# Attention and mixture of experts on one core: waits of TensorE placed ahead of need, the threshold's scalar loaded by GpSimd, ten warming products

## The chip, the cores and the metric

The program runs on one core of one Trainium2 chip, as one launch. The metric is the device time in microseconds (us). Three runs of the kernel before are given, and one profiled execution. An engine is named as in the profile: PE is TensorE (PEld its weight loads), DVE is VectorE, ACT is ScalarE, POOL is GpSimd, SP is SyncE.

## The reference

Attention over 8 batches of 8 heads, 576 tokens of width 64, where scores more than `tau` below the row's maximum are dropped; then a soft mixture of experts over all 4608 tokens (8 experts, 4 slots each, width 512 to 1024 to 512).

```python
scores = scale * np.matmul(q, k.transpose(0, 1, 3, 2))
thresh = np.max(scores, axis=-1, keepdims=True) - tau
scores = np.where(scores >= thresh, scores, -1000000000.0)
attn = softmax(scores)                       # over the keys
x = np.matmul(attn, v)                       # heads side by side: (4608, 512)
logits = x @ phi                             # (4608, 32)
d = softmax(logits, axis=0)                  # over the tokens
slot_input = d.T @ x
slot_out = relu(slot_input @ w1[e]) @ w2[e]  # for each expert e
out = softmax(logits, axis=1) @ slot_out
```

All data is float32.

## The kernel before

**Stages.** At the start, constants are made: GpSimd makes an identity matrix (`ident`, 128x128), SyncE loads the scalar `tau` to all 128 partitions (line 602), and VectorE makes `flag8` (line 604), `nabs` and `pabs` (lines 619 and 621) from it. TensorE multiplies `ident` by itself `UP` = 13 times (line 630); these warming products have no use but to keep TensorE at work while the first data comes in. Then follows the attention, up to about 475 us, and then the experts (lines 1219 and 1254) and the output (lines 1298 and 1304).

**Attention.** The 64 heads go in 32 pairs, four pairs to a batch. For each pair SyncE loads keys, queries and values; of the first pair the halves come from SyncE and ScalarE in turn (lines 745 and 746). The keys are scaled by `flag8` (line 754: VectorE for the first pair, GpSimd later). A pair has nine score rows. For each: TensorE forms 128x576 scores in a PSUM region (`ps`, line 774; the ninth, with the leftover tokens, line 779), VectorE copies them to `ss` and takes the maximum (line 786), ScalarE takes the exponential (line 796), GpSimd the threshold (line 799), VectorE drops what is below it and sums (line 802). Then TensorE transposes the result `p` in pieces of 64 (line 690, `ptr`), ScalarE copies it out to `pTa`, `pTb`, `pTl` (line 695), TensorE multiplies with the values `vv` (line 892), and a turned-back `x` is scaled by GpSimd (line 911) and transposed once more by TensorE (line 916).

**What sets the order.** `Order.add` records each operation with its engine, a planned duration, its needs and its `mode`, the tiling of TensorE's array. `Order.plan` (line 458) simulates the engines from a table of numbers (`TABLE`) and gives every operation a planned start; it also gives out the PSUM regions (four of them) and the buffers. `Order.run` (line 532) then writes the operations in the order of their planned starts, and the program's framework adds the waits: each instruction can carry one wait on a semaphore, and further ones stand in separate rows ahead of it (EVENT_SEMAPHORE in the trace). Before the change all waits of an operation stand at its first instructions. An engine works through its instructions in order.

**Lines of the steps that follow.** The filling products on `ident` in the first pair (line 682) stand among the first score products. The separate waits belong to lines 690, 774, 892 and 916. The operation of line 892 has ten products of 64 rows (256 or 320 columns), that of line 690 mostly sixteen.

Of the kernel before, what the change touches and what calls it, by code (L numbers as in the profile page):

```python
# [10 lines left out]
F32 = mybir.dt.float32  # L11
# [15 lines left out]

HALVES, COLS, COLS4, QUADS, WHOLE = range(5)
SWITCH = 145
PERIOD = 14142.5  # L30

REGIONS = 4
NPRE = 26
UP = 13
WARM = 13
FILL = 14
NHOST = 20
# [362 lines left out]
class Order:  # L400
# [57 lines left out]
    def plan(self, table):  # L458

        ops = self.ops  # L460
        n = len(ops)
        nom = [base * PERIOD / 9 + table.get((name, k), rel * PERIOD / 9) for name, k, base, rel in self.noms]
        left = [len(o[3]) for o in ops]
# [19 lines left out]
        while any(queue.values()):  # L483
# [33 lines left out]
            if eng == "PE":  # L517
                end += SWITCH * (o[5] != mode) + 50 * (free[eng] < t)
                mode = o[5]
# [12 lines left out]
    def run(self, tc):  # L532
        start, slot = self.plan(TABLE)
        self.start = start
        pool = tc.alloc_tile_pool(name="ps", bufs=1, space=PSUM)
        banks = [pool.tile([128, 2, 512], F32, name=f"ps{i}") for i in range(REGIONS)]
        for i in sorted(range(len(start)), key=lambda i: (start[i], i)):
            for b in self.ops[i][4]:
                if b.t is None:
                    k = slot[b]  # L540
                    if b.kind in "sw":
                        b.t = banks[k[0]] if b.kind == "s" else banks[k[0]][:, 0]
                    else:
                        b.t = self.slots[b.kind][k]
            self.ops[i][2]()
        pool.release()
        return slot


@with_exitstack  # L550
def softmax_attention_soft_moe(
# [17 lines left out]
    nc = tc.nc  # L569
# [13 lines left out]
    cp = ctx.enter_context(tc.tile_pool(name="consts", bufs=1))  # L583
    wp = ctx.enter_context(tc.tile_pool(name="weights", bufs=1))
    att = ExitStack()


    ident = cp.tile([128, 128], F32, name="ident")
    make_identity(nc, ident)
    st1 = cp.tile([128, 32], F32, name="st1")  # L590
    nc.vector.tensor_reduce(
        out=st1, in_=ident.rearrange("p (g s) -> p s g", g=4), axis=AX.X, op=ALU.add
# [5 lines left out]
    nc.vector.memset(ones_left[0:64], 0.0)  # L598
    nc.vector.memset(ones_left[64:128], 1.0)
    phi_sb = cp.tile([128, HP, NS], F32, name="phi_sb")  # L600
    tau_sb = cp.tile([128, 1], F32, name="tau_sb")
    nc.sync.dma_start(tau_sb, tau.to_broadcast([128, 1]))
    flag8 = cp.tile([128, 1], F32, name="flag8")
    nc.vector.tensor_scalar(
        out=flag8, in0=tau_sb, scalar1=0.0, scalar2=0.125, op0=ALU.is_ge, op1=ALU.mult
# [21 lines left out]
    with tc.tile_pool(name="ps_up", bufs=1, space=PSUM) as up:  # L627
        t = up.tile([128, 512], F32, name="up")
        for i in range(UP):
            nc.tensor.transpose(out=t[:, i % 4 * 128:i % 4 * 128 + 128], in_=ident, identity=ident)  # L630
# [7 lines left out]
        d=([128, 2, 4, NS], F32), M=([128, 2], F32), f=([128, 1], F32),  # L638
# [19 lines left out]
    n = NPRE + NHOST  # L658
# [459 lines left out]
    start, first_plan = G.plan(TABLE)  # L1118
    slot = first_plan
    users = {}  # L1120
# [3 lines left out]
    end = lambda c: max(start[k] + G.ops[k][1] for k in users[c])  # L1124
# [8 lines left out]
    for i in range(NHOST):  # L1133
        n = next(n for n in reversed(range(len(cells))) if sum(map(bytes_of, cells[n:])) >= (i + 1) * 4096)
        G.add("SP", 1350, NP * N9 + 9, lambda n=n, i=i: host(n, i),
              after=sorted({users[c][-1] for c in cells[n:] if c in users} | {k for c in cells[n:] for k in users.get(c, ()) if k >= recent[-3]}))
    with tc.manual_schedule():
        slot = G.run(tc)
# [182 lines left out]
    end = [None, None]  # L1321
# [75 lines left out]
```

## Time and profile before

| what | value |
|---|---|
| three runs | 546.73, 546.8, 548.49 us (median 546.8) |
| profiled execution | 546.92 us |
| its span, first to last instruction | 545.1 us |
| mean granted clock of TensorE | 0.992 |
| scores, line 774, on TensorE | 166.7 us, 1024 matmuls of 429 ns |
| values, line 892, pTb / pTa / pTl | 76.0 / 62.3 / 41.9 us |
| transpositions of p, line 690 | 98.0 us, 2304 of 223 ns |
| separate waits on TensorE at lines 774, 690, 892, 916 | 74, 59, 32, 28 |

A busy time is the sum over the instructions of a group, and "idle before" is the time that the engine stood still ahead of them. In the timeline each row has its start, how long it lasts, the engine, the line, the operation, and output and input; in brackets stands the idle time before it and what ended it. "SPq" and "ACTq" are the queues' issues of transfers.

### The profile page before, as it was taken

The numbers are of one execution on the slowest core, as the hardware profiler recorded it, in microseconds if no ns is written. First come the engines' busy times: TensorE is split into PE (matmuls) and PEld (weight loads), VectorE is DVE, ScalarE is ACT, GpSimd is POOL, SyncE is SP. The second block draws the span as 40 slices with busy tenths as digits, with TensorE's granted clock in tenths as the row PEclk, the third lists the DMA queues.
The fourth block names the chain that finished last, engine by engine and source line by source line (L and its number), as shares of the span: only waits on it lengthen the run. The fifth ranks groups of instructions, "written<-read, shape, count | busy, mean of one in ns | idle before, by whom it ended". The sixth has DMA issues, their size and how long they took to land.

```text
span 545.1 us, 18237 instructions
## 1 busy us (share of the span) xinstructions
PE 524.6 (96%) x7016; PEld 339.9 (62%) x7016; DVE 473.8 (87%) x1333; ACT 459.5 (84%) x789; POOL 234.1 (43%) x475
## 2 busy tenths in 40 slices
PE   8999999999999999999999999999999999999990
PEld 6666666666666666666766666666666666644470
DVE  6999999999999999999999999998999999623192
ACT  3999998999899989999999989998999989611181
POOL 2554544554345444553455435554564445021030
PEclk9999999999999999999999999999999999999996
DMA  6433335557472738275424333333334223899598
GB/s 154 92 90 92 96 90 189 162 161 182 118 214 85 215 91 244 60 211 129 130 66 117 90 91 93 91 91 92 83 76 114 52 53 130 334 408 407 207 372 320
DMA packets 31990, 83.03 MB, mean 152 GB/s; under 512 B 4640, under 2 KB 12832, under 8 KB 31904
## 3 DMA queue, kind: packets, MB, share of 16 engines
q1 hardware_dynamic: 31584, 81.43, 49.1%
q8 instruction: 55, 0.90, 0.7%
q10 hardware_dynamic: 320, 0.44, 0.3%
q14 instruction: 31, 0.25, 0.1%
HBM read 72.42 MB, written 9.44 MB: 150 GB/s over the span
## 4 chain that ended last, share of the span: by engine, by line
PE 77%; DVE 7%; ACT 6%; DMA 4%; issue 3%; SPq 0%; DVEq 0%; POOL 0%; POOLq 0%; ACTq 0%
PE ps L892 27%; PE ps L774 22%; PE ps L690 16%; PE ps L779 3%; ACT p L796 2%; PE ps L916 2%; DVE ss L786 2%; DMA host<-in_w 2%; DMA w<-in_w 2%; DVE p L802 2%; PE ps L1022 2%; PE ps L974 2%; PE h L1219 1%; ACT pTa L695 1%; DVE host L1308 1%
## 5 line engine op out<-in xcount | busy, mean ns | idle before, releaser
L786 DVE TENSOR_SCALAR_CACHE_REDUCE ss<-ps 128x576 f32<-128x576 f32 x288 | 208.4, 752 | 12.4 <-issue 3.7
L802 DVE SCALAR_TENSOR_TENSOR p<-ss,thr,p 128x576 f32<-128x576 f32 x256 | 206.4, 836 | 2.3 <-POOL thr L799 1.4
L796 ACT ACTIVATE p<-ss,nmx 128x576 f32<-128x576 f32 x256 | 187.5, 775 | 11.0 <-DVE ss L786 10.0
L799 POOL TENSOR_SCALAR thr<-nmx,pabs 128x1 f32<-128x1 f32 x288 | 121.1, 425 | 158.4 <-DVE ss L786 148.8
L774 PE MATMUL ps<-k,q 64*128 64x288 f32 x1024 | 166.7, 429 | 0.7 <-issue 0.2
L774 PEld LDWEIGHTS ps<-k,q 64*128 64x128 f32 x1024 | 84.5, 189 | 25.9 <-ACT pTb L695 4.8
L690 PEld LDWEIGHTS ps<-ident,p 64*128 64x128 f32 x2304 | 88.9, 138 | 18.1 <-DVE ss L786 2.9
L690 PE MATMUL ps<-ident,p 64*128 64x64 f32 x2304 | 98.0, 223 | 0.4 <-ACT pTl L874 0.2
L695 ACT COPY pTb<-ps 128x1024 f32<-128x1024 f32 (+1 forms) x96 | 83.4, 877 | 2.8 <-PE ps L690 2.1
L892 PE MATMUL ps<-pTb,vv 128*64 128x320 f32 x512 | 76.0, 439 | 0.0
L695 ACT COPY pTa<-ps 128x1024 f32<-128x1024 f32 x64 | 64.9, 1015 | 1.3 <-PE ps L690 1.0
L892 PE MATMUL ps<-pTa,vv 128*64 128x256 f32 x512 | 62.3, 385 | 0.2 <-ACT pTa L695 0.2
L892 PEld LDWEIGHTS ps<-pTb,vv 128*64 128x64 f32 x512 | 33.9, 136 | 32.7 <-issue 3.9
L892 PEld LDWEIGHTS ps<-pTa,vv 128*64 128x64 f32 x512 | 33.9, 136 | 25.2 <-DVE ss L786 6.2
L911 POOL TENSOR_TENSOR x<-x,ri 128x512 f32<-128x512 f32 x31 | 34.8, 1122 | 20.0 <-ACT x L695 19.8
L892 PE MATMUL ps<-pTl,vv 128*64 128x256 f32 (+1 forms) x256 | 41.9, 406 | 0.0
L833 POOL TENSOR_SCALAR pL<-pL,ri 128x576 f32<-128x576 f32 x31 | 24.4, 788 | 27.4 <-DVE ri L829 14.5
L695 ACT COPY xT<-ps 128x256 f32<-128x256 f32 (+1 forms) x62 | 24.7, 401 | 5.3 <-PE ps L892 3.5
L802 DVE SCALAR_TENSOR_TENSOR pL<-ss,thr,pL 128x576 f32<-128x576 f32 x32 | 26.1, 816 | 1.5 <-ACT pL L796 1.4
L892 PEld LDWEIGHTS ps<-pTl,vv 128*64 128x64 f32 x256 | 18.4, 137 | 12.7
L695 ACT COPY pTl<-ps 128x256 f32<-128x256 f32 x64 | 23.9, 374 | 2.5 <-PE ps L690 1.8
L754 POOL TENSOR_SCALAR k<-k,flag 128x576 f32<-128x576 f32 x31 | 24.7, 797 | 2.9 <-DMA k<-in_kT 1.7
(166 smaller groups left out, 532.3 us busy)
## 6 DMA issues: line engine op xcount, KB each, us to landing
w<-in_w SPq DMA_DIRECT2D x44, 512.0 KB, 8.4
q<-in_qT SPq DMA_DIRECT2D x62, 288.0 KB, 4.5
vv<-in_vt SPq DMA_DIRECT2D x32, 320.0 KB, 4.2
host<-in_w SPq DMA_DIRECT2D x20, 512.0 KB, 8.5
k<-in_kT SPq DMA_DIRECT2D x62, 144.0 KB, 3.4
out<-w SPq DMA_DIRECT2D x8, 512.0 KB, 3.4
out<-host SPq DMA_DIRECT2D x8, 512.0 KB, 5.1
out<-host SPq DMA_DIRECT2D x4, 256.0 KB, 4.5
```

The source lines that it names most:

```text
L690: nc.tensor.transpose(out=s[:, g, c:c + 64], in_=ins[g], identity=ident[rows[g], rows[g]], tile_position=(64 * g, 0))
L695: G.add("ACT", 51 + 0.833 * n, nom, lambda: nc.scalar.copy(*io()), r, w)
L754: sc = lambda e, kc=kc: lambda: e.tensor_scalar(out=kt.t[:, kc], in0=kt.t[:, kc], scalar1=flag8, **one)
L774: nc.tensor.matmul(s.t[:, g, 0:HS], qt.t[rows[g], h, c * 128:(c + 1) * 128], kt.t[rows[g], h * HS:(h + 1) * HS], start=True, stop=True, ti ...
L779: nc.tensor.matmul(s.t[rows[a], g, 0:HS], qt.t[rows[g], a, SM:S], kt.t[rows[g], a * HS:(a + 1) * HS], start=True, stop=True, tile_position ...
L786: dve(674, t + OFF['mx'], [s], [ss, nmx], lambda s=s, ss=ss, nmx=nmx: nc.vector.tensor_scalar(out=ss.t.rearrange("p (a k) -> p a k", a=2), ...
L796: G.add("ACT", 668, t + OFF['ex'], lambda sv=sv, nmx=nmx, view=view: nc.scalar.activation(view().rearrange("p (a k) -> p a k", a=2), sv(), ...
L799: pool(250, t + OFF['th'], lambda nmx=nmx, thr=thr: nc.gpsimd.tensor_scalar(out=thr.t, in0=nmx.t, scalar1=1.0, scalar2=pabs, op0=ALU.mult, ...
L802: fn=lambda sv=sv, thr=thr, view=view, i=i: nc.vector.scalar_tensor_tensor(out=view().rearrange("p (a k) -> p a k", a=2), in0=sv(), scalar ...
L833: pool(725, t + OFF['sc'], lambda k=k, view=view_: nc.gpsimd.tensor_scalar(out=view(), in0=view(), scalar1=ri.t[:, k:k + 1], **one), [ri[c ...
L892: nc.tensor.matmul(lone(w)[h * 64:(h + 1) * 64, 0:n], vv.t[:, v0:v0 + 64], p0, start=(kb == 0), stop=(kb == 4), tile_position=(0, h * 64), ...
L911: G.add("POOL", 1040, u + 6.8, own=f"new{j}" + group(b), r=[ri[0]], w=[x[j]], fn=lambda: nc.gpsimd.tensor_tensor(out=wide(), in0=wide(), i ...
```

## The change

Three parts. First, `run` now asks a new function, `early`, for waits that are to be taken ahead. For each operation of TensorE it collects the latest need on each other engine and each load, together with the users of the PSUM region or buffer that it takes over. Of these all but the last by plan (all, if a load is among them) may move to one of the eight operations of TensorE before it, the nearest that qualifies: one of at least 400 ns in the plan, with tiling HALVES or COLS, not a score operation, whose middle lies at least 400 ns (3500 for a load) after the planned end of the producer. In that host the wait is put on the third instruction or the next free ones, up to four. Second, the scalar `tau` is loaded by GpSimd as its first work, ahead of `ident`; SyncE's load of it is gone. Third, `UP` is 10.

```diff
+REACH = 8
-UP = 13
+UP = 10
...
     def run(self, tc):
...
-        for i in sorted(range(len(start)), key=lambda i: (start[i], i)):
+        order = sorted(range(len(start)), key=lambda i: (start[i], i))
+        early = self.early(start, slot, order)
+        made, made_of = [], {}
+        nc = tc.nc
+        nc.push_inst_callback(made.append)
+        for i in order:
...
+            del made[:]
             self.ops[i][2]()
+            made_of[i] = [x.name for x in made]
+            at = [x for x in made][2:]
+            for d in early.get(i, ()):
+                names = made_of[d] if self.ops[d][0] == "SP" else made_of[d][-1:]
+                for name in names:
+                    if at:
+                        tc.add_manual_dep(
+                            at.pop(0), name,
+                            mybir.DependencyInfo(mybir.DependencyClass.Sync, mybir.DependencyReason.DATA),
+                            reason="waited for ahead of the operation that needs it")
+        nc.pop_inst_callback()
...
+    def early(self, start, slot, order):
+
+        ops = self.ops
+        pos = {i: n for n, i in enumerate(order)}
+        end = [start[i] + ops[i][1] for i in range(len(ops))]
+        users = {}
+        for i in order:
+            for b in ops[i][4]:
+                users.setdefault(b, []).append(i)
+        behind, there = {}, {}
+        for i in order:
+            for b in ops[i][4]:
+                if b.kind is not None and users[b][0] == i:
+                    unit = ("ps", slot[b][0]) if b.kind in "sw" else (b.kind, slot[b])
+                    if unit in there:
+                        behind.setdefault(i, []).extend(users[there[unit]])
+                    there[unit] = b
+        seen = {}
+        pe = [i for i in order if ops[i][0] == "PE"]
+        out = {}
+        for n, i in enumerate(pe):
+            need = {}
+            for d in [*ops[i][3], *behind.get(i, ())]:
+                e = ops[d][0]
+                if e == "PE":
+                    continue
+                if e == "SP":
+                    if d not in seen:
+                        need["SP", d] = d
+                elif pos[d] > seen.get(e, -1) and pos[d] > pos.get(need.get(e), -1):
+                    need[e] = d
+            late = sorted(need.values(), key=lambda d: end[d])
+            for d in late if any(ops[d][0] == "SP" for d in late) else late[:-1]:
+                margin = 3500 if ops[d][0] == "SP" else 400
+                for h in reversed(pe[max(0, n - REACH):n]):
+                    if ops[h][1] < 400 or ops[h][5] not in (HALVES, COLS) or ops[h][1] in (488, 494):
+                        continue
+                    if pos[d] < pos[h] and end[d] + margin < start[h] + ops[h][1] / 2 and len(out.get(h, ())) < 4:
+                        out.setdefault(h, []).append(d)
+                        break
...
+    tau_sb = cp.tile([128, 1], F32, name="tau_sb")
+    nc.gpsimd.dma_start(tau_sb, tau.to_broadcast([128, 1]))
     ident = cp.tile([128, 128], F32, name="ident")
     make_identity(nc, ident)
...
-    tau_sb = cp.tile([128, 1], F32, name="tau_sb")
-    nc.sync.dma_start(tau_sb, tau.to_broadcast([128, 1]))
```

The order of the products, copies and loads stays what it was on every engine, but for the scalar's load, the three products, and `pabs`, which now stands behind the scaling of the first keys. Three places show what moved. The first is GpSimd's first work, before:

```order
L1383 MEMSET const-uint8-127 128x1
masks.py:197 MEMSET ident 128x128
masks.py:199 ISA
masks.py:199 AFFINE_SELECT ident<-ident 128x128 [waits Pool_49]
L799 TENSOR_SCALAR thr_230<-nmx_290,pabs 128x1 [waits DVE_49]
```

and now (the line numbers are those of the changed file):

```order
L1448 MEMSET const-uint8-127 128x1
L654 DMA tau_sb<-in_tau 128x1
masks.py:197 MEMSET ident 128x128
masks.py:199 ISA
masks.py:199 AFFINE_SELECT ident<-ident 128x128 [waits Pool_49]
L864 TENSOR_SCALAR thr_227<-nmx_287,pabs 128x1 [waits DVE_49]
```

The scalar's load stands ahead of the identity, whose last step releases the warming products. The second place is TensorE around 99.4 us of the profile, in the second batch: the values' product, the transposition of `x` behind it, and the next ones. Before:

```order
L892 MATMUL ps_328<-pTb_194,vv_190 64x320 [waits Activation_49]
L892 MATMUL ps_328<-pTb_194,vv_190 64x320 x7
L892 MATMUL ps_328<-pTl_198,vv_190 64x320 x2
L916 MATMUL ps_326<-ident,x_142 128x64 [waits DVE_49,Pool_49]
L916 MATMUL ps_326<-ident,x_142 128x64 x7
```

and now, the same work (line 957 is what line 892 was, and 981 is 916):

```order
L957 MATMUL ps_325<-pTb_191,vv_187 64x320 [waits Activation_49]
L957 MATMUL ps_325<-pTb_191,vv_187 64x320
L957 MATMUL ps_325<-pTb_191,vv_187 64x320 [waits DVE_49]
L957 MATMUL ps_325<-pTb_191,vv_187 64x320 x5
L957 MATMUL ps_325<-pTl_195,vv_187 64x320 x2
L981 MATMUL ps_323<-ident,x_139 128x64 [waits Pool_49]
L981 MATMUL ps_323<-ident,x_139 128x64 x7
```

The wait for VectorE, which reads the PSUM region that the transposition takes over, has moved from the transposition to the third of the ten products before it. The third place follows a microsecond later: the first score product with a new pair's keys and queries. Before:

```order
L690 MATMUL ps_325<-ident,p_266 128x64 [waits Activation_49]
L690 MATMUL ps_325<-ident,p_266 128x64 x15
L774 MATMUL ps_328<-k_254,q_258 128x288 [waits DMAHW1_49,DMAHW0_49,Activation_49]
L774 MATMUL ps_328<-k_254,q_258 128x288 [waits DMAHW2_49]
L774 MATMUL ps_326<-k_254,q_258 128x288 [waits Activation_49]
```

and now (line 755 is what line 690 was, and 839 is 774):

```order
L755 MATMUL ps_322<-ident,p_263 128x64 [waits Activation_49]
L755 MATMUL ps_322<-ident,p_263 128x64
L755 MATMUL ps_322<-ident,p_263 128x64 [waits DMAHW7_49]
L755 MATMUL ps_322<-ident,p_263 128x64 [waits DMAHW0_49]
L755 MATMUL ps_322<-ident,p_263 128x64 [waits DMAHW1_49]
L755 MATMUL ps_322<-ident,p_263 128x64 [waits DMAHW7_49]
L755 MATMUL ps_322<-ident,p_263 128x64 x10
L839 MATMUL ps_325<-k_251,q_255 128x288 [waits Activation_49]
L839 MATMUL ps_325<-k_251,q_255 128x288
L839 MATMUL ps_323<-k_251,q_255 128x288 [waits Activation_49]
```

The waits for loads (DMAHW) have moved into the transposition ahead of the scores, one to a product. In the whole listing TensorE has 785 products that wait before and 961 now, and of these 204 carried more than one wait before and 83 now.

More of the change, by code (lines that the diff above doesn't have):

```diff
@@ L546, in run @@
+        nc.pop_inst_callback()
         pool.release()
         return slot
+    def early(self, start, slot, order):
[37 more added lines that the diff above has]
+                        break
+            for d in need.values():
+                if ops[d][0] == "SP":
+                    seen[d] = True
+                else:
+                    seen[ops[d][0]] = max(seen.get(ops[d][0], -1), pos[d])
+        return out
```

## The prediction

> **What bounds the kernel now.** I read the page first, then the chain of work that ended last, then who waited for whom.
>
> ```profile
> span 545.1 us, 18237 instructions
> ...
> PE 524.6 (96%) x7016; PEld 339.9 (62%) x7016; DVE 473.8 (87%) x1333; ACT 459.5 (84%) x789; POOL 234.1 (43%) x475
> ...
> PE 77%; DVE 7%; ACT 6%; DMA 4%; issue 3%; SPq 0%; DVEq 0%; POOL 0%; POOLq 0%; ACTq 0%
> ```
>
> ```profile
> PE ps L779 <- ACT pTl L874: 1.8, 5, 0.4
> ```
>
> TensorE is busy for 96% of the span and carries 77% of the chain, so time that TensorE loses in the attention part is lost to the kernel, and only time that it now loses can be won. The list of waits names little of that: the longest entry for a TensorE product is 1.8 us in five pieces, where the 64x64 products of line 779 wait for a ScalarE copy. That wait comes last where it stands, and the change does not touch its producer.
>
> The first 9 us are another matter, since there nothing else runs yet. The timeline of the start, and the first link of the chain:
>
> ```profile
> 0.73 0.20 POOL masks.py:197 MEMSET ident<- 128x128 f32 x1 [0.29 <-POOLq L1383]
> 0.73 0.40 SPq L602 DMA_DIRECT2D tau_sb<-in_tau  x1
> ...
> 1.01 0.29 POOL masks.py:199 TENSOR_SCALAR_AFFINE_SELECT ident<-ident 128x128 f32<-128x128 f32 x1
> ...
> 1.19 0.58 SPq L745 DMA_DIRECT2D k<-in_kT  x1
> ...
> 1.36 3.04 PE L630 MATMUL up<-ident 128*128 128x128 f32 x13 [1.36 <-POOL ident masks.py:199]
> 1.81 0.59 SPq L746 DMA_DIRECT2D q<-in_qT  x1
> ...
> 2.44 0.60 SPq L745 DMA_DIRECT2D k<-in_kT  x1
> ...
> 3.33 0.15 DVE L604 TENSOR_SCALAR flag<-tau_sb 128x1 f32<-128x1 f32 x1 [1.71 <-DMA tau_sb<-in_tau]
> ...
> 4.11 0.37 DVE L754 TENSOR_SCALAR k<-k,flag 128x288 f32<-128x288 f32 x1 [0.32 <-DMA k<-in_kT]
> ...
> 4.46 0.69 PE L682 MATMUL ps<-ident 128*128 128x128 f32 x2
> ...
> 5.23 2.37 PEld L774 LDWEIGHTS ps<-k,q 64*128 64x128 f32 x12 [0.49 <-issue]
> ...
> 6.31 0.37 DVE L754 TENSOR_SCALAR k<-k,flag 128x288 f32<-128x288 f32 x1 [1.83 <-DMA k<-in_kT]
> ...
> 6.88 0.75 DVE L786 TENSOR_SCALAR_CACHE_REDUCE ss<-ps 128x576 f32<-128x576 f32 x1
> ```
>
> ```profile
> 2.44 3.77 DMA k<-in_kT
> 6.96 1.42 DVE ss L786 x4
> ```
>
> The chain begins with the keys of the second half, issued by SyncE at 2.44 and landed at 2.44 + 3.77 = 6.21. VectorE scales them at 6.31, sums the identity, and starts the first maximum at 6.88. TensorE's first score products start at 5.23, just after the two filling products (4.46 + 0.69 = 5.15). So three paths reach the start together: SyncE's loads, the warming products, and the threshold's scalar (flag at 3.33, scaled keys at 4.11).
>
> **The separate waits.** A product can carry one wait; where it needs more, a row of its own (EVENT_SEMAPHORE) stands ahead of it. By line:
>
> ```profile
> L774 PEldq EVENT_SEMAPHORE  x74: 51/51/1348, 5.2 to 449.8; - x74
> ...
> L892 PEldq EVENT_SEMAPHORE  x32: 51/51/716, 18.6 to 464.9; - x32
> ...
> L916 PEldq EVENT_SEMAPHORE  x28: 51/51/51, 32.2 to 452.6; - x28
> ...
> L690 PEldq EVENT_SEMAPHORE  x59: 51/51/51, 22.1 to 470.8; - x59
> ```
>
> Nearly all take 51 ns. In the program's listing 204 products had several waits, now 83: 121 lose the row ahead of them, and at most 121 x 0.051 = 6.2 us could go with it. Does such a row cost the product behind it anything? The same operation, pTa's product with vv, once followed by a transposition that has one wait (76.21) and once by one that has two (105.80):
>
> ```profile
> 76.21 1.95 PE L892 MATMUL ps<-pTa,vv 128*64 128x256 f32 x16
> ...
> 78.52 0.65 PE L690 MATMUL ps<-ident,p 64*128 64x64 f32 x14
> ```
>
> ```profile
> 105.80 1.95 PE L892 MATMUL ps<-pTa,vv 128*64 128x256 f32 x16
> ...
> 108.11 0.52 PE L690 MATMUL ps<-ident,pL 64*128 64x64 f32 x10
> ```
>
> From start to start it is 78.52 - 76.21 = 2.31 and 108.11 - 105.80 = 2.31 us. The row is worked off while older products still run. So I cost the removed rows at **nothing**; the work that hides them is the long operation in front, and if that cover were gone it would be 51 ns each. Only rows whose own wait comes last cannot be hidden, and the rule keeps most of those: it moves a wait only where the plan has the producer done 0.4 us before the host's middle. The changed listing still has two waits, of ScalarE and GpSimd, on many transpositions of pL.
>
> **What the earlier waits cost.** A wait now stands on the third product of a host operation, and everything behind it on TensorE stands still until it is met. The critical place is the one shown in the listing above, which returns in each batch: L916 needs VectorE's maximum, and that wait moves to the third product of the L892 operation before it.
>
> ```profile
> 99.11 0.75 DVE L786 TENSOR_SCALAR_CACHE_REDUCE ss<-ps 128x576 f32<-128x576 f32 x1
> 99.79 0.08 DVE L786 DVE_READ_ACCUMULATOR ss<-ps 128x1 f32 x1
> ```
>
> ```profile
> 99.70 0.14 PEld L892 LDWEIGHTS ps<-pTb,vv 128*64 128x64 f32 x2
> ```
>
> ```profile
> 99.38 2.37 PE L892 MATMUL ps<-pTb,vv 128*64 128x320 f32 x16
> 101.59 0.71 PE L892 MATMUL ps<-pTl,vv 128*64 128x320 f32 x4
> 102.23 0.46 PE L916 MATMUL ps<-ident,x 64*128 64x64 f32 x8
> ```
>
> VectorE ends at 99.79 + 0.08 = 99.87; the weight load of the third product started at 99.70, so it comes 0.17 us later. The pairs of matmuls stand (101.59 - 99.38) / 8 = 0.28 us apart, so the load runs that far ahead of its matmul and most of the 0.17 is cover. Bounds: 0, and 0.17 with nothing hidden; I take **0.05 us**, near the lower end, because the pitch of this row is the larger number. Eight batches make 0.4 us, bounds 0 and 1.4. A gain below nothing would need the separate rows to cost something, which the 2.31 against 2.31 excludes here. The other moved waits are mostly loads of k and q, whose producers ended long before.
>
> **The start.** Taken from SyncE's queue, the scalar's issue frees 1.19 - 0.73 = 0.46 us: keys and queries that SyncE issues move up by as much, the second half's keys from 2.44 to 1.98, and with them the scaling at 6.31 and the maximum at 6.88. Against that GpSimd now issues a transfer before it makes the identity. No row shows GpSimd issuing one. Bounds: 0, and the whole time from issue to landing of this transfer; the nearest row is SyncE's issue of the same bytes, 0.40 us, and I take that, d = **0.40**.
>
> ```profile
> tau_sb<-in_tau SPq DMA_DIRECT2D x1, 0.5 KB, 2.6
> ```
>
> ```profile
> L630 PE MATMUL up<-ident x13: 421/421/477, 1.4 to 4.0; 128*128 128x128 f32 x13
> ```
>
> The warming products start at 1.36 + d. All 13 take 3.04 us and the last of them 0.42, so they start (3.04 - 0.42) / 12 = 0.22 apart, and three fewer save 0.65. The filling products then end at 5.15 - 0.65 + d, and the first score product can load 0.08 later as before: 4.58 + d = 4.98 instead of 5.23, **-0.25 us**. The scalar would land at 0.73 + d + 2.6 = 3.7; the flag (0.15) and the scaling of the first keys (0.37) behind it end near 4.4, which the warming still hides, the more since the changed program scales the first keys ahead of pabs. At d = 0 the loads decide, -0.46, SyncE's share; at d = 2.6 it is +1.95. The page DMA: Bandwidth & Descriptors of the Trainium skill (section Specifications) gives the path through GpSimd about 1 us to the first byte and that of SyncE about 0.6; with its 1 us as d the first score product would start at 5.58, +0.35. No run here shows it yet.
>
> **Sum.** -0.25 + 0.4 = +0.15 us against the profiled execution's 546.92 (its span is 545.1; the rest lies around it, and the median of the three runs is 546.8): **547.1 us**, no change. Less than 0.3%, 1.64 us, cannot be told from no change.
>
> **The rivals.**
> 1. *The separate rows are in the way after all.* Then up to 6.2 us go: 540.7; a third of it passes the bound. For it speaks that there are so many and that they stand on the busiest engine; against it the two equal 2.31. Chance 0.15.
> 2. *The identity comes late (slower).* Place: GpSimd's first work. Past d = 0.65 every further 0.1 us puts TensorE's first score product 0.1 us later. With the 0.4 of the hosts it passes 1.64 us from d = 0.65 + 1.24 = 1.89; at the upper bound of 2.6 the time is 546.9 + 1.95 + 0.4 = 549.3. For it speaks that nothing else can run on GpSimd meanwhile, against it the 0.40 of the nearest row. Chance 0.07.
> 3. *The change does not take waits off but adds stalls.* The plan's times choose the hosts, not the chip's. With nothing hidden, 8 x 0.17 = 1.4, and the smaller places as much again: 549.3 to 549.7 with all of them, 548.7 with half. Against it: the load's lead. Chance 0.06.
> 4. *TensorE's clock opens later.* The score products of the start need twice the time of the next ones:
>
> ```profile
> 5.20:7.30 2.10, 2.04 (x8) 2.07 (x10) 1.00 0.94 250
> 8.30:9.50 1.20, 1.15 (x8) 0.69 (x8) 1.00 0.94 243
> ```
>
> Eight matmuls in 2.04 us, then eight in 1.15, while both windows show a granted clock of 1.00. A later first product can lengthen the slow stretch, and each us of it loses about half a us. One of the three runs lies 548.49 - 546.73 = 1.76 above the lowest; one such step would give 546.9 + 1.8 = 548.7. Chance 0.05. The page TensorE: Matmul & The Clock Gate of the Trainium skill (Part 1: The HAM clock gate) says that the clock opens at the end of a busy window of about 3.4 us that runs by itself; an estimate by it is 1.7 us for one window more. The halved rate agrees with it; no run here shows the windows.
>
> **How the numbers follow.** Forecast 0.67, rivals 0.15, 0.07, 0.06, 0.05. Faster by over 0.3% is the first rival, 0.15; slower are the other three, 0.18; the same is 0.67. The range begins at 545.0, where part of the first rival still lies, and ends at 548.7, which takes in the clock's step and half of the stalls; the full gain and the late identity are left out.
>
> **What would show it.** The separate rows on lines 774 and 892 gone, and still 2.31 us from L892 to the next operation: the first term is right; a smaller step speaks for the first rival. A gap in the weight loads of the third product near 99.9: the second term, its size against 0.05. The start of the first warming product gives d; the first score product should start near 5.0, the first maximum before 6.88. Wrong would be a first score product after 5.9, or a batch whose length, from one L892 row to the same one of the next batch, has changed by over 0.1 us.

## The result and the profile after

Seven runs of each kernel, medians 553.01 us (548.25 to 555.61) after and 547.07 us (546.56 to 548.87) before: the ratio is 1.0088, with a 95% interval of 1.0062 to 1.0114. The change makes the kernel slower by 5 to 6 us, and 547.1 was forecast with 548.7 as the upper end.

The profiled execution of the changed kernel is the shortest of its seven, 548.25 us. Its page, span, busy times, the chain by engine, and the one new queue:

```profile
span 546.5 us, 18103 instructions
PE 524.5 (96%) x7013; PEld 337.3 (62%) x7013; DVE 473.7 (87%) x1333; ACT 459.3 (84%) x789; POOL 233.3 (43%) x476
PE 74%; DMA 9%; ACT 6%; DVE 4%; issue 3%; POOL 1%; SPq 0%; DVEq 0%; POOLq 0%; ACTq 0%
q0 software_dynamic: 32, 0.00, 0.0%
```

TensorE's busy time has not moved (524.6 before). What has grown is the DMA part of the chain, from 4 to 9%. Most of the rows ahead of the products are gone as meant, 216 before and 86 now: by line, with their counts,

```profile
L839 PEldq EVENT_SEMAPHORE  x6: 51/51/51, 5.9 to 450.0; - x6
L755 PEldq EVENT_SEMAPHORE  x48: 51/51/51, 58.5 to 471.1; - x48
L957 PEldq EVENT_SEMAPHORE  x1: 51/51/51, 465.9 to 465.9; - x1
```

against 74 (now line 839), 59 (755) and 32 (957) before. The timeline of TensorE and of its weight loads at the places that the prediction measured (line 957 is what line 892 was):

```profile
75.69 1.95 PE L957 MATMUL ps<-pTa,vv 128*64 128x256 f32 x16
...
78.00 0.71 PE L755 MATMUL ps<-ident,p 64*128 64x64 f32 x16
```

```profile
105.30 1.95 PE L957 MATMUL ps<-pTa,vv 128*64 128x256 f32 x16
...
107.61 0.53 PE L755 MATMUL ps<-ident,pL 64*128 64x64 f32 x10
```

```profile
98.87 2.38 PE L957 MATMUL ps<-pTb,vv 128*64 128x320 f32 x16
101.08 0.71 PE L957 MATMUL ps<-pTl,vv 128*64 128x320 f32 x4
101.72 0.46 PE L981 MATMUL ps<-ident,x 64*128 64x64 f32 x8
```

```profile
99.42 1.27 PEld L957 LDWEIGHTS ps<-pTb,vv 128*64 128x64 f32 x12 [0.35 <-DVE ss L851]
```

From 75.69 to 78.00 it is still 2.31 us, but this place had one wait before and has one now. The place that had a separate row is the second: before, the row stood at 106.17 and the step was 2.31 us; now the trace has no row there, and from 105.30 to 107.61 it is 2.31 us again. At 99.42 the third product's weight load waits 0.35 us for VectorE's maximum, and yet the operation takes 101.72 - 98.87 = 2.85 us, as before (102.23 - 99.38): the wait is hidden whole.

The start, in the timeline:

```profile
0.74 0.60 SPq L810 DMA_DIRECT2D k<-in_kT  x1
...
1.26 0.74 POOL L654 DMA_DIRECT2D tau_sb<-in_tau  x1 [0.81 <-POOLq L1448]
...
2.00 0.22 POOL masks.py:197 MEMSET ident<- 128x128 f32 x1
...
2.64 2.40 PE L695 MATMUL up<-ident 128*128 128x128 f32 x10 [2.64 <-POOL ident masks.py:199]
...
6.05 1.45 PE L839 MATMUL ps<-k,q 64*128 64x288 f32 x9 [0.26 <-DMA q<-in_qT]
...
7.05 0.74 DVE L851 TENSOR_SCALAR_CACHE_REDUCE ss<-ps 128x576 f32<-128x576 f32 x1
```

GpSimd begins the scalar's load 0.53 us after it could begin the identity before (0.73), and issues it for 0.74: the identity is later by 2.00 - 0.73 = 1.27 us. The first score product starts at 6.05 instead of 5.23, the first maximum at 7.05 instead of 6.88.

TensorE's products come in the same order in both kernels, so I paired them one by one, counted from the end, and took the difference of their starts. In this execution it is -0.6 us at 25 us (the trace's clock record begins, at full speed, at 5.7 us here and at 7.3 before), and it then loses 0.3 at 177.6, 0.3 at 422 and about 0.9 in the experts' part, to 1.4 at the end. That is not the loss of the other six runs. A second profile was needed.

### The profile page after: what moved, and what is told of

It is laid out like the page before. It is cut to its first block, busy times and chain, and to the rows that moved or that the text cites. A ratio compares the mean times of both kernels' runs of the same rounds, so it can differ in the third digit from the quotient of the medians.

```text
span 546.5 us, 18103 instructions
## 1 busy us (share of the span) xinstructions
PE 524.5 (96%) x7013; PEld 337.3 (62%) x7013; DVE 473.7 (87%) x1333; ACT 459.3 (84%) x789; POOL 233.3 (43%) x476
## 4 chain that ended last, share of the span: by engine, by line
PE 74%; DMA 9%; ACT 6%; DVE 4%; issue 3%; POOL 1%; SPq 0%; DVEq 0%; POOLq 0%; ACTq 0%
PE ps L957 26%; PE ps L839 23%; PE ps L755 16%; DMA host<-in_w 4%; DMA w<-in_w 4%; PE ps L844 3%; PE ps L981 2%; ACT p L861 2%; PE ps L1039 1%; PE ps L1087 1%; DVE ss L851 1%; ACT pTa L760 1%; DVE host L1373 1%; DMA vv<-in_vt 1%; DVE cT L1276 1%
## 5 line engine op out<-in xcount | busy, mean ns | idle before, releaser
L864 POOL TENSOR_SCALAR thr<-nmx,pabs 128x1 f32<-128x1 f32 x288 | 119.8, 421 | 159.2 <-DVE ss L851 149.8
L839 PEld LDWEIGHTS ps<-k,q 64*128 64x128 f32 x1024 | 83.4, 188 | 26.3 <-ACT pTb L760 4.9
```

Source lines behind the costliest of these rows:

```text
L839: nc.tensor.matmul(s.t[:, g, 0:HS], qt.t[rows[g], h, c * 128:(c + 1) * 128], kt.t[rows[g], h * HS:(h + 1) * HS], start=True, stop=True, ti ...
L864: pool(250, t + OFF['th'], lambda nmx=nmx, thr=thr: nc.gpsimd.tensor_scalar(out=thr.t, in0=nmx.t, scalar1=1.0, scalar2=pabs, op0=ALU.mult, ...
```

## The experiments

The kernels are taken in three groups of four, each group beside new runs of the kernel before, whose medians are 547.56, 547.47 and 547.96 us. A ratio is that of a kernel to the kernel before of its group, with its 95% interval.

### The changed kernel once more

No edit.

> The changed kernel once more, for a second profile: the one there is (548.25 us) lies 4 to 7 us below the other six runs of the same kernel, so it does not show where most of the loss is. Every theory expects a median near 553. Theory A (the start): GpSimd's first transfer took 1.27 us before the identity in the first profile; in the other runs it takes some 5 us more, so the first score product starts near 11 instead of 6.05 us, and everything behind it is shifted by the same amount. Theory B (the waits): the start is as before, and the loss adds up in the attention part, in steps where a product of a long operation waits. Theory C (the weight stream): start and attention are as before up to 470 us, and the products of the last part wait 5 us longer for their weights.

553.8 us, ratio 1.0113 (1.0088 to 1.0139), and the profiled run is 554.29. The page's span, and from the waits of TensorE the first row; then TensorE's timeline:

```profile
span 552.4 us, 18103 instructions
...
PE ps L755 <- DMA vv<-in_vt: 3.2, 2, 2.5
```

```profile
176.96 0.47 PE L755 MATMUL ps<-ident,pL 64*128 64x64 f32 x10
177.26 0.35 PE L755 MATMUL ps<-ident,p 64*128 64x64 f32 x6
180.09 1.01 PE L755 MATMUL ps<-ident,p 64*128 64x64 f32 x14 [2.48 <-DMA vv<-in_vt]
181.03 1.24 PE L844 MATMUL ps<-k,q 64*64 64x288 f32 x8
```

The same place in the kernel before:

```profile
177.60 0.79 PE L690 MATMUL ps<-ident,p 64*128 64x64 f32 x20
178.32 0.71 PE L779 MATMUL ps<-k,q 64*64 64x288 f32 x8
178.97 1.95 PE L892 MATMUL ps<-pTa,vv 128*64 128x256 f32 x16
```

An operation of twenty transpositions stops after six, for a load of values that no transposition reads. Before, that wait stood at the product with vv, 178.97 - 177.60 = 1.37 us later. The windows around it (engines' busy time, then the granted clock, the DMA share and GB/s):

```profile
170.00:177.50 7.50, 7.50 (x102) 4.95 (x100) 6.98 (x21) 7.36 (x12) 5.04 (x9) 1.00 0.66 203
177.50:180.00 2.50, 0.11 (x4) 0.00 (x0) 2.50 (x9) 2.45 (x6) 1.34 (x4) 0.98 1.06 235
180.00:182.50 2.50, 2.41 (x24) 1.42 (x26) 0.78 (x3) 1.73 (x3) 0.00 (x0) 0.50 0.67 186
182.50:185.00 2.50, 2.50 (x20) 1.32 (x16) 1.34 (x4) 0.00 (x0) 0.69 (x1) 0.84 0.03 13
```

TensorE stands still, and when it goes on the clock is at 0.50: the trace's clock record has one stretch of 3.41 us at half speed here. So the place costs twice. By pairs of products against the profile of before: start -0.45; the stop 2.75; the half clock 1.35; a stop of the same kind at 239 us (vv again, 0.69 in the waits) 0.88; two steps of 0.12; the experts' part 2.2; the rest to the last instruction 0.36. Together 7.3 us, the difference of the spans (552.4 - 545.1). Theory A falls (the start even gained), B and C have a part each.

### One part alone

The waits alone: `UP` and the scalar's load are put back.

```diff
-UP = 10
+UP = 13
...
-    tau_sb = cp.tile([128, 1], F32, name="tau_sb")
-    nc.gpsimd.dma_start(tau_sb, tau.to_broadcast([128, 1]))
...
+    tau_sb = cp.tile([128, 1], F32, name="tau_sb")
+    nc.sync.dma_start(tau_sb, tau.to_broadcast([128, 1]))
```

> The waits taken ahead alone; the scalar stays with SyncE, 13 warming products. Theory A: 546.5 to 547.5, as before. Theory B: 551 to 553. Theory C, if the scalar's queue is the cause: as before. The prediction's own terms for this part: +0.4 (547.3).

549.35 us, 1.0033 (1.0016 to 1.0050): above theory A's range and below theory B's, and 2 us above the prediction's own 547.3. TensorE stands still for vv at 178 here too, 0.9 us.

GpSimd's load alone, in the kernel before:

```diff
+    tau_sb = cp.tile([128, 1], F32, name="tau_sb")
+    nc.gpsimd.dma_start(tau_sb, tau.to_broadcast([128, 1]))
     ident = cp.tile([128, 128], F32, name="ident")
...
-    nc.sync.dma_start(tau_sb, tau.to_broadcast([128, 1]))
```

> The scalar's load by GpSimd alone, 13 warming products, no waits ahead. Theory A: 551 to 554, with the first warming product some 5 us later in those runs. Theory B: d = 1.27 less the 0.46 of SyncE and not the 0.65 of the warming, about 547.5 to 548. Theory C: 551 to 553, and the products of line 1219 or its counterpart wait for weights.

547.36 us, 0.9999 (0.9984 to 1.0015): nothing, though the first warming product comes 1.28 us later (2.64).

Ten warming products alone, in the kernel before:

```diff
-UP = 13
+UP = 10
```

> 10 warming products instead of 13, nothing else. All three theories: 546.5 to 547, since the first score products wait for the queries that land at 5.1. If the clock opens a window later with less warming: 548 to 549.

548.2 us, 1.0017 (1.0006 to 1.0028): the second case of the expectation, a clock that opens later. In its profile the clock record begins at 9.9 us instead of 7.3, and the products are 1.33 us behind those of before at 10 us and 1.35 at 170. The three parts alone add up to 1.8 - 0.2 + 0.6 = 2.2 us; together they cost 6.2. Something in them multiplies.

### Two parts, and the load waits put back

Waits on loads stay at the product that needs them; everything else as changed:

```diff
-            for d in late if any(ops[d][0] == "SP" for d in late) else late[:-1]:
+            for d in [d for d in late if ops[d][0] != "SP"] if any(ops[d][0] == "SP" for d in late) else late[:-1]:
```

> The changed kernel, but waits on loads (126 of the 179 that the rule moves) stay at the product that needs them; the 53 on engines are still taken ahead. Theory V (a load of vv lands after the product that now waits for it: 2.5 us of standing still near 177.5 and 0.7 us near 235 in the second profile of the changed kernel, a half-speed window of the clock behind the first): without these places 546.5 to 548.5, and the difference from before stays under 0.5 us between 170 and 240 us. Theory E (the waits on engines stall as well): 549 to 551. Theory S (the new start costs 3 us or more by itself): 550 or more.

548.58 us, 1.0015 (1.0000 to 1.0029), a little above theory V's 548.5, and no step between 170 and 215 us in the pairing. The profiled execution (549.12) loses 1.85 us up to 25 us (its clock record begins at 11.7), and from there to 400 us only 0.2: the waits on engines cost next to nothing. With 553.8 for all three parts, the waits on loads carry nearly 5 us of the loss; those on engines, with the start, about 1.

The start alone: GpSimd's load and `UP = 10` in the kernel before.

> The scalar by GpSimd and 10 warming products, no waits taken ahead. Theory V: 547 to 548 (alone the two parts gave 547.4 and 548.2). Theory S: 550 to 552, the two parts together costing what neither does alone.

547.96 us, 1.0010 (0.9995 to 1.0025): in theory V's range, and theory S falls.

The waits and GpSimd's load (the changed kernel with `UP = 13`), and the waits with ten products (the scalar with SyncE):

> The waits taken ahead and the scalar by GpSimd, with 13 warming products. The waits alone gave 549.35, all three 553.8. If GpSimd's load is the part that makes the waits dearer: 552 to 554. If the ten products are: 549 to 550.

> The waits taken ahead and 10 warming products, the scalar with SyncE. If the ten products make the waits dearer: 552 to 554. If GpSimd's load does: 549 to 550.5.

549.22 us, 1.0035 (1.0016 to 1.0053), and 553.65 us, 1.0119 (1.0065 to 1.0174, four runs from 550.5 to 557.86). It is the ten products that make the waits dear, 170 us and more after the last of them has run. In the profile of the second (557.86, its longest run) TensorE stands for vv 3.3 us near 179, and the clock is at half speed for 6.83 us behind it.

### Why three products matter at 177 us

A load raises its semaphore sixteen times, and TensorE waits for the sixteenth. The Trainium skill's page DMA: Bandwidth & Descriptors (Why a DMA increments its semaphore by 16 and not by 1) says that each of up to sixteen DMA engines adds one when its own share is done; the trace agrees, with sixteen rises for each load. The chain of waits gives the load's whole time in the two profiles of the changed kernel, first the short run, then the long one:

```profile
172.67 4.91 DMA vv<-in_vt
177.58 0.04 issue
177.63 0.65 PE ps L755 x14
```

```profile
172.80 7.24 DMA vv<-in_vt
180.04 0.04 issue
180.09 1.01 PE ps L755 x13
```

In the second, fifteen shares had landed by 177.35 and the last came at 180.04: one DMA engine was 2.7 us behind. The profile's rows of queues name what else goes over the DMA engines:

```profile
q8 instruction: 55, 0.90, 0.7%
q14 instruction: 31, 0.25, 0.2%
```

The first row is 55 pieces of 16 KB. TensorE has 14115 rows in the trace, 257 for each piece, and no other engine has over 2000: so I take these as TensorE's instructions on their way to it. A piece is fetched when TensorE has come so far in its list: in all fourteen profiles the eighteenth piece starts when TensorE has begun between 4508 and 4563 of its rows. A shorter list moves each later fetch to a later place in the work. From the trace's records of packets and semaphores, for the vv load near 173 to 174 us (us; the fetch's start counts from the issue of the load):

```
kernel                    fetch starts  takes   15th, 16th share   TensorE stood
before                       -2.03      0.96    177.82  177.84        -
waits + GpSimd, UP 13        +0.09      1.22    178.90  179.26       0.6
waits, UP 13                 +0.13      1.05    178.54  178.76       0.9
changed, short run           +0.77      1.21    176.77  177.58       0.3
waits, UP 10                 +1.06      2.48    178.63  182.47       3.3
changed, long run            +1.58      1.69    177.35  180.04       2.5
```

With 13 products the fetch starts just as the load is issued, with 10 about 1 us later, in the midst of the 2.5 MB that SyncE sends off there (two loads each of k, vv, q and w). Then one share falls far behind the others, and that begins with the loads behind the fetch: in the waits with `UP` 10 the load of keys just ahead of them has its sixteenth share 0.25 us behind the fifteenth, the weight load that follows 3.33 and the vv load 3.84. Three products are six rows (a weight load and a matmul each), or 0.2 us at TensorE's mean pace, so the list's length alone does not give the whole 1 us; what adds the rest is open. To see whether it is the list's length, I gave three products back elsewhere, and took three away elsewhere, among the filling products near 9 us, where the warming is over (the first edit in the waits with `UP` 10, the second in the waits with `UP` 13; SyncE loads the scalar in both):

```diff
-        G.add("PE", 218, 500 if i else -100, lambda i=i: [tr(fill.t[:, k * 128:k * 128 + 128], ident) for k in (i % 2 * 2, i % 2 * 2 + 1)],
+        G.add("PE", 218, 500 if i else -100, lambda i=i: [tr(fill.t[:, k * 128:k * 128 + 128], ident) for k in [i % 2 * 2, i % 2 * 2 + 1] + [0, 1, 2] * (i == 5)],
```

> The waits taken ahead with 10 warming products (553.65 us without more), and three more products of the same kind among the ten filling products near 9.4 us, so that TensorE's list of instructions is as long up to 170 us as with 13 warming products. Theory F (what counts is where in TensorE's list a 16 KB piece of its instructions is fetched: in the two slow profiles it moves over one DMA engine while the vv load does, at 174.4 and 175.4, and that engine ends 2.7 and 3.8 us after the other fifteen): 549 to 550, as with 13. Theory U (less warming as such, or the later start): 552 to 554.

549.82 us, 1.0034 (1.0018 to 1.0049): with 10 warming products and the long list the time is that of 13. The fetch starts at +0.23, takes 1.15, and TensorE stands 0.6 us.

```diff
-        G.add("PE", 218, 500 if i else -100, lambda i=i: [tr(fill.t[:, k * 128:k * 128 + 128], ident) for k in (i % 2 * 2, i % 2 * 2 + 1)],
+        G.add("PE", 218, 500 if i else -100, lambda i=i: [tr(fill.t[:, k * 128:k * 128 + 128], ident) for k in [i % 2 * 2, i % 2 * 2 + 1][i in (4, 5, 6):]],
```

> The waits taken ahead with 13 warming products (549.35 us), and three filling products fewer near 9.4 us: TensorE's list is as long as with 10 warming products. Theory F: 552 to 554, and one of the sixteen engines ends the vv load near 177 us over 2 us late in the profile, if the profiled execution is such a one. Theory U: 549 to 550.

551.48 us, 1.0081 (1.0049 to 1.0113), less than the 552 to 554 of theory F, but above the 549.35 of the same warming with the long list, and above theory U's 550. In its profile the fetch starts at +1.13 and takes 2.03, fifteen shares land by 176.65 and the last at 180.13:

```profile
176.91 0.35 PE L755 MATMUL ps<-ident,p 64*128 64x64 f32 x6
180.17 0.65 PE L755 MATMUL ps<-ident,p 64*128 64x64 f32 x14 [2.91 <-DMA vv<-in_vt]
```

```profile
180.20:184.50 4.30, 4.30 (x38) 2.50 (x40) 1.56 (x6) 1.17 (x2) 0.69 (x1) 0.68 0.32 99
```

So the length of TensorE's list counts, not the warming: with ten products and with thirteen, the kernel with the longer list is the faster one (with thirteen the two intervals just touch). That the long warming with the short list is 2 us below the 553.65 of the short warming is not told apart (the intervals overlap). That the fetch goes over the very DMA engine that is late, and makes it late, is argued from the times: the records don't name the engine. And the short run of the changed kernel had the fetch at +0.77 with only 0.8 us of lateness: why the same program is sometimes spared stays open.

### Which loads

Only the 32 waits on vv are put back (147 moved waits remain):

```diff
+            vv = lambda d: any(b.kind == "vv" for b in ops[d][4]) and ops[d][0] == "SP"
+            for d in [d for d in late if not vv(d)] if any(ops[d][0] == "SP" for d in late) else late[:-1]:
```

> The changed kernel, but the 32 waits on loads of vv stay at the product that needs them; the other 147 are taken ahead. Theory V (the loss over 548 is the loads of vv): 547.5 to 549, as with no wait on loads taken ahead (548.58). If the loads of k and q stall as much: 550 to 553.

548.53 us, 1.0010 (0.9991 to 1.0030), as with no load wait moved.

The rule keeps a larger distance, which puts back 7 of the 126:

```diff
-                margin = 3500 if ops[d][0] == "SP" else 400
+                margin = 6000 if ops[d][0] == "SP" else 400
```

> The changed kernel with a rule that asks for 6 us between the end of a load's issue in the plan and the product that waits early, instead of 3.5: 7 of the 126 load waits (5 of them on vv) go back to the product that needs them. Theory V, with the loss at the few places where the plan has no more than 3.5 us: 547.5 to 549. If the loss is spread over all load waits: 551 to 554.

549.54 us, 1.0039 (1.0020 to 1.0059), between the two theories: the few tight places (in the kernel's plan the five loads of vv have 3.9 to 4.9 us; three of the five are the places of the stops at 177, 239 and 422 us) hold over 4 of the 6 us, and its profile shows no stop for vv. The 1 us above 548.5 is within the intervals. Both edits change the length of the list as well, so a part of their gain may be a fetch that falls elsewhere; the two were not separated. No version here beats the kernel before, so none was sought further.

## Why the prediction was wrong, point by point

- **The separate rows cost nothing.** Right: 2.31 us with the row and without it, and rival 1 falls. With 130 rows fewer no profile gains in the attention; with the vv waits put back, the difference from before goes from 1.25 us at 25 us to 1.41 at 400, and rival 1 had up to 6.2 us to win.
- **The host of line 892 (now 957) ahead of 916 (now 981).** 0.05 us was taken; it is 0.00 at the place measured (2.85 and 2.85), though the weight load waits 0.35 us, twice the 0.17 of the working: it runs far enough ahead to hide all of it. All waits on engines together, loads left in place, stand at 548.58 against 547.96 for the start alone: 0.6 us and not distinguishable from nothing, where the sum had 0.4.
- **"The other moved waits are mostly loads of k and q, whose producers ended long before."** This step failed. 126 of the 179 moved waits are on loads, 32 of them on vv, and I priced them at nothing without the landing of a single one. The page of before had the row that speaks against it:

```profile
vv<-in_vt SPq DMA_DIRECT2D x32, 320.0 KB, 4.2
```

  The rule asks for 3.5 us from the planned end of the issue to the host's middle; from issue to landing the median is already 4.2, and with the fetch in the way 7.2 to 8.1 us. In the trace of before the load near 173.8 us landed at 177.84, after its host had started (177.60) and 1.1 us ahead of the product that needs it (178.97): a wait at the host's first products was already too early in that very trace. In the runs it cost 0.3 to 3.3 us of standing still, and 1.35 to 1.6 us for each 3.41 us of half clock.
- **Rival 3** (the plan's times choose the hosts, not the chip's) is what happened, at 0.06 and with a wrong price: its 1.4 us came from VectorE's 0.17 us, and the loads were left out of it. By its own figures half of its 2.8 us gives 548.3, not the 548.7 that stands there.
- **The start.** d = 0.40 was taken from SyncE's row; it is 1.27, within the bounds (0 to 2.6) but three times the value, since GpSimd both begins later and issues for longer. The first score product starts at 6.05, past the 5.9 named as wrong, and it waits for the queries by then, not for the warming. The size was wrong and the sign too (-0.25 forecast), but the whole start costs 0.5 us with an interval through 0 (1.0010, 0.9995 to 1.0025): the first maximum moves by 0.17 only.
- **The three products** were costed by their time alone. That fewer instructions move the fetches of all later ones was no term and no rival.
- **The clock.** Rival 4 looked for it in the start, and it shows there too. In six of the nine profiles with ten products the clock record begins, at full speed, at 9.1 to 11.7 us, and the products are 1.3 to 2.5 us behind those of before at 10 us; in the other three it begins at 5.7 to 6.0, and in all five with thirteen at 4.3 to 8.7. The prediction's granted 1.00 for 5.20 to 7.30 us was no measurement: the record of before has no entry ahead of 7.3, and the view then shows 1.00. With one or two profiles for each kernel, how often the clock opens late is not shown. The larger loss of clock came 170 us later, when TensorE had stood still for 2.5 us or more: one stretch of 3.41 us at half speed in two profiles, 6.83 in a third, and none behind stops of 0.3 to 0.9 us. The Trainium skill's page TensorE: Matmul & The Clock Gate (HAM oscillation — how this bites in real kernels) says that a wait for a transfer which crosses the clock's window makes the next products run cold; the trace agrees, with 0.50 in the row of 180.00 to 182.50. Its example has waits of 3 to 5 us; here 2.5 us were enough.
- **The experts' part.** No term stood for it; it lost 0.9 and 2.2 us in the two profiles of the changed kernel. In the second the last share of a weight load lands 1.4 us behind the other fifteen (496.67 and 495.23), which before was 0.2. The trace shows where that begins: the load that lands at 486.29 is 0.07 us behind, the next, at 488.99, 1.43, and between them a piece of TensorE's instructions is fetched (486.7, 1.11 us). With the waits and `UP` 10 it is the same, 0.24 and 1.78 on the two sides of the fetch at 489.5. Other fetches there leave a smaller step or none, and no run took one away, so this too is argued from the times; the 0.9 us of the first profile stays open.

## What to carry to other kernels

A wait moved ahead of its need moves a deadline, so each one is priced by when its producer ends on the chip, loads first: take the landing from the trace at that place, not its median and not the plan's. On the engine that bounds the kernel an early wait on a load stops work that does not need it, and a stop can also halve the clock behind it (those of 2.5 to 3.3 us did here, those of 0.9 us and less did not). And where several parts together cost more than the sum of each alone, change the length of the instruction list by itself, with a few idle products: here six instructions, 170 us before the stop, were worth 2 to 4 us.

## What was not expected of the hardware

- TensorE's instructions come in over the DMA engines that carry the data, 16 KB at a time, 55 times, a median of 1.1 us each and up to 2.5 us; in three profiles one share of a load under way at such a fetch landed 2.7 to 3.8 us behind the other fifteen.
- GpSimd's issue of a 0.5 KB load took 0.74 us and began 0.53 us late, where SyncE's took 0.40. The identity behind it was late by 1.27 us.
